# Opening order, score banks and one turn of the first rows in an attention and mixture-of-experts kernel

## The chip, the cores and the metric

The kernel runs as one program on one core of a Trainium2 chip. The metric is device microseconds from launch to end, the median of several executions. TensorE (PE) multiplies and turns tiles, VectorE (DVE) and ScalarE (ACT) work on the results, GpSimd (POOL) helps with elementwise work and starts the indirect transfers, and SyncE (SP) starts nearly all others. Each engine has a list of instructions of its own and takes them in that order.

## The reference

Three stages follow each other, all in float32. Shapes: 4 batches of 576 tokens, 8 heads of 64, so 2304 rows of 512 numbers between the stages.

```python
# windowed attention: a key counts where 0 <= rel < 128
scores = (q @ k.T) / sqrt(64) + slopes[head] * (-abs(rel));  masked: -1e9
attn = exp(scores - max); attn /= sum + 1e-9;  x = attn @ v
# dense layer over 2304 rows, 512 -> 2048 -> 512
h = x @ w_in;  x = (h - tanh(h)) @ w_out
# experts: 8, one for each row, 512 -> 1024 -> 512
xn, en = x / norm(x), expert_emb / norm(expert_emb)
logits = xn @ en.T / tau;  expert = argmax;  gate = softmax[expert]
out = gate * (relu(x @ w1[expert]) @ w2[expert])
```

## The kernel before

The 2304 rows are 18 blocks of 128, two blocks to a group, nine groups. Attention runs by block and, within it, by four quarters of two heads each: scores on PE into two score banks (`sc0`, `sc1`, one for each head), masking, bias and row minimum on DVE (`soft`), the exponential on ACT, then a turn of the probabilities, and the product with the values (`pv`). The first four blocks ("early", 16 quarters) are all float32: their probabilities are turned on PE through the one `misc` bank (`tr_pe`, L526), copied out (`tr_out`) and multiplied by `pv_f` (L540). Block 0 has one key block, so its scores are 128 wide, the others' 256. Later blocks use split operands and a transposing DMA instead (L520, L551).

When a block's four quarters are there, `x_out` turns its 512 numbers per row on PE (L642, four 128x128 turns) and writes a high part (ACT) and a low part (DVE, L655) into one of four `xT` slots. The dense layer runs in steps of two tiles of 128 hidden units: 24 matrix products of 256 columns for the first matrix (`g1`, L695), tanh, subtraction, a split into `gh` and `gl` (two sets of buffers, by the parity of the step), and 12 products of 512 columns for the second (`g2`, L719), which add up in the banks `acc0` and `acc1`. There are 72 steps.

Group 0 is visited twice. In the first visit it does four of its eight steps, since the weights are still arriving; its partial sums go out to memory (`spill`). Then group 1 does all eight, and group 0 comes back for the other four. For that return the kernel before has stored group 0's attention rows in memory (`px`, L651), reads them back (L637) and turns them again (`x_out` with `back=True`).

The order on each engine comes from a planner (`Plan.order`). Every task has an engine or a choice of two, a cost per engine, a due time, and keys that it reads and writes. The planner picks the task that can start first by its own costs; ties go to the earlier due time. It allows only one user of `misc` at a time. What the planner assumes is not what the chip does; only the order that results is in the program.

The opening is set by due times: the bias table's source `tmp` at -20, constants and expert embeddings at -9, then queries, keys and values of block 0. `emb` loads the eight expert embeddings, sums their squares on DVE (`sq`, L269), takes a power on POOL (L285), scales them on DVE (L273 to L275), turns them on PE (L280), copies them out and splits them on POOL. `consts` makes eight bias tables on DVE (L240), one for each head. `qk_early` loads queries and keys of the first four blocks; there the keys of block 1 are loaded for block 1 and again for block 2, and those of block 2 again for block 3, so that two key blocks always lie side by side. `weight` loads a 512 KB weight tile (planned at `WLOAD`) and rebuilds float32 from it on DVE and ACT.

Of the kernel before, what the change touches and what calls it, by code (L numbers as in the profile page):

```python
# [10 lines left out]
F32 = mybir.dt.float32  # L11
# [14 lines left out]
DM = H * D  # L26
FF = 2048
E = 8
# [6 lines left out]
FT = FF // 128  # L35
# [4 lines left out]
NF = 4  # L40
WLOAD = 1.46
LOENG = {"DVE": 0.69}
# [3 lines left out]
N0 = 1  # L46
NPX = 16
ALPHA = 1.0
RATE = 0.5
# [115 lines left out]
class Builder:  # L165
# [64 lines left out]
    def consts(self, P):  # L230
        nc, i = self.nc, self.i
        at = {}

        def tmp(e):
            at[0] = self.at.tile([128, 512], F32, tag="xr", name="tmp", bufs=1)
            nc.sync.dma_start(out=at[0][:, 0:384], in_=i["c_bias"])

        P.add({"SP": 0.55}, tmp, -20, w=[("xr", m) for m in range(4)])
        for h in range(H):
            P.add({"DVE": 0.2}, lambda e, h=h: nc.vector.tensor_scalar(  # L240
                out=self.bias[:, h, :], in0=at[0][:, 0:256], scalar1=2.0 ** -(h + 1), scalar2=None, op0=ALU.mult),
                -20 + h, r=[("xr", 0)], w=[("bias", h)])
        P.add({"POOL": 0.5}, lambda e: nc.gpsimd.tensor_copy(out=self.tri, in_=at[0][:, 256:384]), -11,
              r=[("xr", 0)], w=["tri"])
# [14 lines left out]
    def emb(self, P, due):  # L259
        nc = self.nc  # L260
        ss = self.rt.tile([E, 1], F32, name="ess")

        def load(e):
            self.ec2 = self.at.tile([128, 512], F32, tag="pt0", name="ec", bufs=1)[0:E, :]
            nc.sync.dma_start(out=self.ec2, in_=self.i["emb"])

        def sq(e):
            junk = self.at.tile([128, 512], F32, tag="pt1", name="sq", bufs=1)[0:E, :]
            nc.vector.tensor_tensor_reduce(out=junk, in0=self.ec2, in1=self.ec2, scale=1.0, scalar=0.0,  # L269
                                           op0=ALU.mult, op1=ALU.add, accum_out=ss)  # L270
# [13 lines left out]
        P.add({"DVE": 0.6}, sq, due, r=["ec", ("pt", 0), "at"], w=["ess", ("pt", 1)])  # L284
        P.add({"POOL": 0.6}, lambda e: nc.gpsimd.tensor_tensor(out=ss, in0=ss, in1=self.half[0:E], op=ALU.pow), due,  # L285
              w=["ess"], r=["small"])
        P.add({"DVE": 0.8}, norm, due, w=["ess", "ec"], r=[("pt", 0), "at"])
        P.add({"PE": 0.5}, tr, due, r=["ec", ("pt", 0), "con", "at"], w=["eps"], take="misc")
        P.add({"DVE": 0.1}, lambda e: nc.vector.tensor_copy(
# [17 lines left out]
    def weight(self, P, kind, f, due):  # L307
# [6 lines left out]
        v = {}  # L314
# [18 lines left out]
        def lo(e):  # L333
# [5 lines left out]
                 ("o", FT - 4): [("qf", 2), ("qf", 3)]}.get(key, [])  # L339
        if kind == "o" and 1 <= FT - f < NF:  # L340
            slots = [("kf", FT - f, 0), ("kf", FT - f, 1)]
        P.add({"SP": WLOAD}, load, due - 2, w=[raw] + slots)
# [49 lines left out]
    def qk_early(self, P, b, due):  # L392

        nc, d2 = self.nc, b // 2

        def load_k(e):
            t = max(b, 1)
            if b != 1:
                self.kf[t] = self.wp.tile([128, 2, 4, 128], F32, tag=f"wo{FT - t}", name=f"kf{t}")
# [8 lines left out]
        P.add({"SP": 0.73}, load_q, due, r=["at"], w=[("qf", b)] + ([] if b % 2 else [("qf", b + 1)]))  # L408
        P.add({"SP": 0.73 if b < 2 else 1.46}, load_k, due, r=["at"],
              w=[("kf", 1, 0)] if b == 1 else [("kf", max(b, 1), 0), ("kf", max(b, 1), 1)])  # L410

# [31 lines left out]
    def quarter(self, P, a, due):  # L443
# [11 lines left out]
        sk = (a // 2) % 2  # L455

        def scores(jj):
            sc = v["sc"][jj] = self.scores[jj]
            j = qq + 2 * jj
            hp, p0 = hf * 4 + j, 64 * jj  # L460
            if early:
                x = slice(1, 2) if one else slice(0, 2)
                nc.tensor.matmul(sc[:, 0:W // 128, :], lhsT=self.qf[b // 2][p0:p0 + 64, b % 2, hf * 2 + qq, :],
                                 rhs=self.kf[max(b, 1)][p0:p0 + 64, x, hf * 2 + qq, :], start=True, stop=True)
                return
# [126 lines left out]
        for jj in range(2):  # L592
            if early:
                P.add({"PE": 0.3 if one else 0.42}, lambda e, jj=jj: scores(jj), due,
                      r=["at", ("qf", b)] + [("kf", max(b, 1), x) for x in ([1] if one else [0, 1])], w=[("sc", jj)])
            else:
                P.add({"PE": 0.11 if one else 0.22}, lambda e, jj=jj: scores(jj), due,
                      r=["at"] + ks + [("kl", x, hf) for x in kv] + q, w=[("sc", jj)])
        for jj in range(2):
            P.add({"DVE": ttr}, lambda e, jj=jj: soft(jj), due, r=["at", ("bias", qd * 2 + jj)],  # L600
                  w=[("sc", jj), ("mx", jj, a % 2)])
        for jj in range(2):
            P.add({"ACT": 0.57 if one else 0.67}, lambda e, jj=jj: exp(jj), due,
                  r=["at", ("sc", jj), ("mx", jj, a % 2)], w=[("p32", pb, jj), ("sm", sk, qq, jj)])
        sm = [("sm", sk, x, y) for x in range(2) for y in range(2)]
# [23 lines left out]

    def x_out(self, P, b, s, due, back=False):  # L630

        nc = self.nc
        v = {}

        def reload(e):
            t = self.xr[b] = self.at.tile([128, DM], F32, tag="xr", name="xr", bufs=1)
            nc.sync.dma_start(out=t, in_=self.px[b])  # L637

# [607 lines left out]
    def build(self):  # L1246
# [5 lines left out]
        self.bucket = dp.tile([ROWS, ROW], F32, name="bucket")  # L1252
        self.px = dp.tile([2 * N0, 128, DM], F32, name="px")
        self.pa = dp.tile([2 * N0, 128, DM], F32, name="pa")
# [4 lines left out]
        self.consts(P)  # L1259
        self.small_loads(P, -9)  # L1260
        self.emb(P, -9)
        all_f = list(range(FP))
# [12 lines left out]
        for g, fps in visits:  # L1275
# [226 lines left out]
```

## Time and profile before

| what | value |
|---|---|
| time, median of three runs | 810.32 us (808.01 to 810.85) |
| the profiled execution, its span | 813.71 us, 812.0 us |
| PE, its weight loads | 775.1 us (95%), 684.4 us (84%) |
| DVE, ACT, POOL | 569.6 us (70%), 422.0 us (52%), 227.1 us (28%) |
| data moved | 118.90 MB |

A row of the timeline gives the start in us, the duration in us, the engine, the line in the program, the operation, the result and its operands, their shapes and the number of instructions merged into the row; in brackets stands how long the engine had been idle and whose end let it go on. PE's ends are modelled, and neighbouring products overlap; the price of one is therefore read from its start to the start of the next row. A float32 product is two instructions.

### The profile page before, as it was taken

What the parts mean: (1) busy time and instruction counts of PE and PEld (TensorE: products, weight loads), DVE (VectorE), ACT (ScalarE), POOL (GpSimd) and SP (SyncE); (2) the same over time, 40 slices, a digit from 0 to 9 for tenths busy, and PEclk for the clock granted to TensorE, in tenths of its full rate; (3) what the DMA queues carried; (4) which work ended last, traced back from release to release, by engine and by line L of the source; (5) the groups of instructions that cost most, each with busy time, mean ns of one, the idle gap of its engine ahead of it and who ended that gap; (6) DMA issues with size and microseconds to landing.
All of it is one profiled execution on the core that took longest, in us unless ns stands there. A gap on an engine that the chain in (4) does not pass through costs nothing. (4 is left out here: it accounts for less than half of the span.)

```text
span 812.0 us, 15246 instructions
## 1 busy us (share of the span) xinstructions
PE 775.1 (95%) x5225; PEld 684.4 (84%) x5225; DVE 569.6 (70%) x1544; ACT 422.0 (52%) x953; POOL 227.1 (28%) x242
## 2 busy tenths in 40 slices
PE   6999999988999998999999999989999999999995
PEld 4688998886888987888988989978879899989894
DVE  5788988968587697788787886776456665756420
ACT  4787866555354455555555643555246554545220
POOL 2113034646253145144242422321100211210210
PEclk9999999999999999999999999999999999999998
DMA  8896079666245335445364442474167666655100
GB/s 306 312 365 229 34 211 271 139 129 136 65 93 132 82 86 117 105 98 119 84 130 112 73 79 53 153 211 143 66 217 231 202 208 202 198 184 184 40 29 30
DMA packets 128264, 118.90 MB, mean 146 GB/s; under 512 B 87973, under 2 KB 92069, under 8 KB 128048
## 3 DMA queue, kind: packets, MB, share of 16 engines
q1 hardware_dynamic: 125152, 108.37, 48.7%
q0 software_dynamic: 3024, 9.46, 3.2%
q8 instruction: 43, 0.70, 0.4%
q14 instruction: 45, 0.37, 0.2%
HBM read 86.84 MB, written 17.08 MB: 128 GB/s over the span
## 5 line engine op out<-in xcount | busy, mean ns | idle before, releaser
L695 PE MATMUL h<-xT,wi 128*128 128x256 f32 x1728 | 225.5, 284 | 0.0
L695 PEld LDWEIGHTS h<-xT,wi 128*128 128x128 f32 x1728 | 217.0, 191 | 5.9 <-issue 1.3
L719 PE MATMUL acc<-wo,gh 128*128 128x512 f32 x576 | 184.8, 402 | 0.3 <-DVE x2row L759 0.3
L719 PE MATMUL acc<-wo,gl 128*128 128x512 f32 x288 | 113.8, 395 | 0.0
L719 PEld LDWEIGHTS acc<-wo,gh 128*128 128x128 f32 x576 | 100.0, 189 | 15.1 <-DVE x2row L759 0.5
L700 ACT ACTIVATE t<-h 128x512 f32<-128x512 f32 x72 | 43.1, 599 | 103.2 <-PE h L695 98.2
L1129 PE MATMUL y<-eo,ge 128*128 128x512 f32 x336 | 88.8, 399 | 0.5 <-ACT ge L1110 0.5
L505 ACT ACTIVATE p<-sc,mx 128x256 f32<-128x256 f32 (+1 forms) x128 | 59.3, 465 | 41.5 <-DVE mx L491 37.7
L1154 POOL DMA_INDIRECT out<-yo,ix x23 | 24.4, 1059 | 188.1 <-ACT yo L1150 39.8
L491 DVE CUSTOM_DVE_ANT_0 sc<-sc,bias 128x256 f32<-128x256 f32 (+1 forms) x144 | 52.6, 371 | 28.5 <-PE sc L469 19.6
L1129 PEld LDWEIGHTS y<-eo,ge 128*128 128x128 f32 x336 | 59.5, 188 | 10.8 <-ACT ge L1110 0.8
L712 DVE TENSOR_TENSOR gl<-t,gh 128x512 fp32r<-128x512 f32 x72 | 64.9, 902 | 4.9 <-ACT gh L708 4.3
L1027 DVE TENSOR_TENSOR eo<-est,eo 128x512 fp32r<-128x512 f32 x61 | 44.9, 738 | 28.8 <-ACT eo L1023 28.1
L719 PEld LDWEIGHTS acc<-wo,gl 128*128 128x128 f32 x288 | 54.4, 189 | 12.6 <-DVE gl L712 0.5
L1023 ACT CAST eo<-est 128x512 fp32r<-128x512 f32 x64 | 39.6, 620 | 37.1 <-PE y L1125 21.3
L1116 DVE SCALAR_TENSOR_TENSOR ge<-he,ge 128x256 fp32r<-128x256 f32 x104 | 28.7, 316 | 41.2 <-ACT ge L1110 41.2
L1094 PEld LDWEIGHTS he<-xA,ei 128*128 128x128 f32 x384 | 54.2, 188 | 2.5
L1094 PE MATMUL he<-xA,ei 128*128 128x288 f32 (+2 forms) x384 | 56.1, 295 | 0.0
L703 DVE TENSOR_TENSOR t<-h,t 128x512 f32<-128x512 f32 x72 | 49.4, 686 | 9.3 <-ACT t L700 9.1
L1110 ACT ACTIVATE ge<-he 128x288 fp32r<-128x288 f32 (+2 forms) x56 | 23.1, 415 | 62.9 <-PE he L1094 58.7
L1094 PEld LDWEIGHTS he<-xT,ei 128*128 128x128 f32 x384 | 53.4, 189 | 2.1
L1094 PE MATMUL he<-xT,ei 128*128 128x288 f32 (+2 forms) x384 | 54.8, 295 | 0.0
(202 smaller groups left out, 1312.1 us busy)
## 6 DMA issues: line engine op xcount, KB each, us to landing
est<-in_w SPq DMA_DIRECT2D x128, 256.0 KB, 3.2
rawi<-in_w_in SPq DMA_DIRECT2D x16, 511.8 KB, 6.9
rawo<-in_w_out SPq DMA_DIRECT2D x16, 511.8 KB, 5.0
stk<-in_k SPq DMA_DIRECT2D x30, 256.0 KB, 2.9
stq<-in_q SPq DMA_DIRECT2D x28, 256.0 KB, 3.1
bucket<-in_c_pad SPq DMA_DIRECT2D x8, 771.0 KB, 6.3
xe<-bucket SPq DMA_DIRECT2D x17, 257.0 KB, 3.5
vst<-in_v SPq DMA_DIRECT2D x30, 128.0 KB, 2.4
```

The costliest lines, as they stand in the source:

```text
L491: nc.vector.tensor_tensor_reduce(out=x, in0=x, in1=self.bias[:, h, c0:c1], scale=-0.125, scalar=mx[:, 1:2] if m else 3.0e38, op0=ALU.add, ...
L505: nc.scalar.activation(out=v["p32"][:, jj * W:(jj + 1) * W], in_=x, func=AF.Exp, scale=-1.0, bias=v["mx"][jj][:, 0:1], accum_out=self.sums ...
L695: nc.tensor.matmul(h3(v["h"], f2), lhsT=w[:, a, k, :], rhs=xT[c][:, :, k, :], start=(k == 0 and n == 0), stop=(k == KD - 1 and n == 2))
L700: nc.scalar.activation(out=v["t"], in_=v["h"].rearrange("p a b -> p (a b)"), func=AF.Tanh)
L703: nc.vector.tensor_tensor(out=v["t"], in0=v["h"].rearrange("p a b -> p (a b)"), in1=v["t"], op=ALU.subtract)
L712: self.eng(e).tensor_tensor(out=v["gl"], in0=v["t"], in1=v["gh"].bitcast(F32), op=ALU.subtract)
L719: nc.tensor.matmul(self.acc[g, t], lhsT=v[a][:, c0:c0 + 128], rhs=self.w["o", fs[f2]][:, c, :], start=(first and f2 == 0 and n == 0), stop ...
L1023: nc.scalar.copy(out=t[:, 0, :], in_=v["x"])
L1027: self.eng(eng).tensor_tensor(out=t[:, 1, :], in0=v["x"], in1=t[:, 0, :].bitcast(F32), op=ALU.subtract)
L1094: nc.tensor.matmul(h[:, 0:N], lhsT=w[:, a, c0:c0 + 128], rhs=xT()[b][:, k, 0:N], start=(k == 0 and n == 0), stop=(k == KD - 1 and n == 2))
L1116: nc.vector.scalar_tensor_tensor(out=g[:, o:o + c1 - c0], in0=hk[f][:, c0:c1], scalar=0.0, in1=g[:, c0:c1].bitcast(F32), op0=ALU.max, op1= ...
L1129: nc.tensor.matmul(y[t], lhsT=gt(f, a)[:, (t - ts[0]) * 128:(t - ts[0] + 1) * 128], rhs=self.w["o", f0 + f][:, b, :], start=(f == 0 and n ...
```

## The change

Seven edits stand together.

1. Group 0's rows are turned once. The `xT` slots of its first visit are still intact at its return, so the store, the reload and the second turn go.
2. The first queries and keys are loaded first (due -25), ahead of `tmp`; the constants come with due -19.
3. `emb` is no longer called at the start but in the loop over blocks, behind `x_out` of block 0, with due 0. Its scratch is now the `gh` and `gl` buffers of odd steps. The call stands under `if b == 0`, not under `if g not in seen`.
4. Two bias tables stay on DVE; the other six go to POOL.
5. In the first eight quarters every second one has its scores in the banks `acc0` and `acc1`.
6. The early keys are loaded once each. Block 1 and 3 still find their two key blocks side by side; block 2 does not, so each of its eight score products becomes two of 128 columns.
7. `WLOAD` goes from 1.46 to 1.28, and some buffer keys follow the new key layout.

```diff
-WLOAD = 1.46
+WLOAD = 1.28
+NALT = 8
...
-            P.add({"DVE": 0.2}, lambda e, h=h: nc.vector.tensor_scalar(
+            P.add({"DVE": 0.2} if h < 2 else {"POOL": 0.5}, lambda e, h=h: self.eng(e).tensor_scalar(
...
-            self.ec2 = self.at.tile([128, 512], F32, tag="pt0", name="ec", bufs=1)[0:E, :]
+            self.ec2 = self.m1.tile([128, 512], F32, tag="gh1", name="ec", bufs=1)[0:E, :]
...
-        P.add({"SP": 0.2}, load, due, w=["ec", ("pt", 0)], r=["at"])
+        ec = [("gh", 1), ("gl", 1)]
+        P.add({"SP": 0.2}, load, due, r=[("xT", 0)], w=ec)
...
-            for x in ([b] if b < 2 else [b, b - 1]):
-                nc.sync.dma_start(out=self.kf[t][:, t - x], in_=self.i["k0"][x])
+            nc.sync.dma_start(out=self.kf[d2][:, 1 - b % 2], in_=self.i["k0"][b])
...
+        P.add({"SP": 0.73}, load_q, -25 if b == 0 else due, r=["at"], w=both("qf"))
+        P.add({"SP": 0.73}, load_k, -25 if b == 0 else due, r=["at"], w=both("kf"))
...
+        bank = "acc" if a < NALT and a % 2 else "sc"
+
         def scores(jj):
-            sc = v["sc"][jj] = self.scores[jj]
+            sc = v["sc"][jj] = self.scores[jj] if bank == "sc" else self.psA.tile(
+                [128, 2, 128], F32, tag=f"acc{jj}", name="scx", bufs=1)
...
+                kt = [self.kf[x // 2][p0:p0 + 64, 1 - x % 2, hf * 2 + qq, :] for x in ([b] if one else [b, b - 1])]
+                if b % 2 and not one:
+                    kt = [self.kf[b // 2][p0:p0 + 64, :, hf * 2 + qq, :]]
+                for m, k in enumerate(kt):
+                    out = sc[:, 0:2, :] if b % 2 and not one else sc[:, m, :]
+                    nc.tensor.matmul(out, lhsT=self.qf[b // 2][p0:p0 + 64, b % 2, hf * 2 + qq, :], rhs=k, start=True,
+                                     stop=True)
...
-        if back:
-            P.add({"SP": 0.73}, reload, due - 2, r=["at", ("px", b)], w=xr)
-        elif b < 2 * N0:
-            P.add({"SP": 0.73}, lambda e: nc.sync.dma_start(out=self.px[b], in_=self.xr[b]), due, r=["at"] + xr,
-                  w=[("px", b)])
...
-        self.emb(P, -9)
+        self.small_loads(P, -19)
...
-                self.x_out(P, b, sl[n], -5 if g in seen else d0 + 4 * rate, g in seen)
+                if g not in seen:
+                    self.x_out(P, b, sl[n], d0 + 4 * rate)
+                if b == 0:
+                    self.emb(P, 0)
```

On PE the program opens so before (`sc` are the score banks, `p` and `p32x` the probabilities of even and odd quarters, `of` the product with the values):

```order
L463 MATMUL sc_97<-kf_135,qf_132 128x128
L463 MATMUL sc_98<-kf_135,qf_132 128x128
L463 MATMUL sc_97<-kf_135,qf_132 128x128
L280 MATMUL misc<-con,ec 128x8 x4
L463 MATMUL sc_98<-kf_135,qf_132 128x128
L526 MATMUL misc<-con,p_167 128x128 x2
L463 MATMUL sc_97<-kf_135,qf_132 128x128
L540 MATMUL of<-vf_140,ptf 128x128 x2
L526 MATMUL misc<-con,p32x 128x128 x2
L463 MATMUL sc_98<-kf_135,qf_132 128x128
```

And so now, with `scx` for the banks that it borrows:

```order
L470 MATMUL sc_97<-kf_132,qf_130 128x128
L470 MATMUL sc_98<-kf_132,qf_130 128x128
L470 MATMUL scx<-kf_132,qf_130 128x128 x2
L470 MATMUL sc_97<-kf_132,qf_130 128x128
L533 MATMUL misc<-con,p_160 128x128 x2
L470 MATMUL sc_98<-kf_132,qf_130 128x128
L470 MATMUL scx<-kf_132,qf_130 128x128 x2
L547 MATMUL of<-vf_138,ptf 128x128 x2
L533 MATMUL misc<-con,p32x 128x128 x2
L470 MATMUL sc_97<-kf_132,qf_130 128x256
```

The turn of the embeddings has gone from here. The second quarter's scores follow the first's at once, and the first turn of probabilities has one head's scores of the third quarter ahead of it.

On POOL the opening reads so before (the row named ISA stands where the trace shows MODIFY_POOL_CONFIG, a setting-up of POOL; `tri` is a constant, `ess` the embeddings' norms):

```order
L253 MEMSET thr 1x8 x16
L243 CAST tri<-tmp 128x128
L285 ISA
L285 TENSOR_TENSOR ess<-ess,half 8x1
L297 CAST en_89<-enT 128x4x8
```

And so now:

```order
L254 MEMSET thr 1x8 x16
L241 ISA
L241 TENSOR_SCALAR bias<-tmp 128x256 x6
L244 CAST tri<-tmp 128x128
L371 TENSOR_TENSOR khl<-stk,khl 64x512 x2
```

The setup row stands ahead of the six bias tables, and the power has moved behind other work.

In group 0's second visit PE has this behind the first GEMM of its third step now; the rows before hold no L280 there:

```order
L693 MATMUL h<-xT_65,wi_1192 128x256
L693 MATMUL h<-xT_64,wi_1192 128x256
L281 MATMUL misc<-con,ec 128x8 x4
L476 MATMUL sc_97<-khl,qst_1634 128x256 x2
L476 MATMUL sc_98<-khl,qst_1634 128x256 x2
L693 MATMUL h<-xT_64,wi_1246 128x256
```

So the embeddings are loaded, normalised and turned a second time. From the second half of step 30 (of 0 to 71) to the end of the program PE's order is the same in both kernels.

## Rows read from the trace of the kernel before

**Rows 1.** Windows: stretch, then busy us of PE, PEld, DVE, ACT, POOL; PEclk; DMA.

```profile
10.16:31.81 21.65, 20.71 (x76) 14.27 (x76) 12.76 (x47) 12.71 (x39) 4.73 (x8) 1.00 0.96 360
41.28:100.00 58.72, 58.72 (x397) 51.57 (x396) 51.79 (x107) 47.68 (x100) 10.10 (x9) 1.00 0.57 213
199.90:205.90 6.00, 4.29 (x24) 3.36 (x24) 2.54 (x6) 0.62 (x1) 1.47 (x1) 0.72 0.02 5
```

**Rows 2.** Timeline of all engines, the opening until the first exponentials.

```profile
0.86 0.40 SPq L236 DMA_DIRECT2D tmp<-in_c_bias  x1
1.78 0.43 SPq L401 DMA_DIRECT2D kf<-in_k  x1
...
3.35 1.80 DVE L240 TENSOR_SCALAR bias<-tmp 128x256 bf16<-128x256 f32 x8 [1.28 <-DMA tmp<-in_c_bias]
...
6.57 0.68 DVE L269 CUSTOM_DVE_ANT_0 sq<-ec 8x512 f32<-8x512 f32 x1 [1.42 <-DMA ec<-in_emb]
...
7.18 0.28 DVE L491 CUSTOM_DVE_ANT_0 sc<-sc,bias 128x128 f32<-128x128 f32 x1
...
7.92 0.36 ACT L505 ACTIVATE p<-sc,mx 128x128 f32<-128x128 f32 x1
```

**Rows 3.** Timeline of PE alone, from the first scores to the 34th microsecond.

```profile
5.76 0.80 PE L463 MATMUL sc<-kf,qf 64*128 64x128 f32 x4 [5.76 <-DMA kf<-in_k]
...
8.92 0.59 PE L280 MATMUL misc<-con,ec 8*128 8x8 f32 x4
...
10.16 0.69 PE L526 MATMUL misc<-con,p 128*128 128x128 f32 x2
...
12.51 0.64 PE L526 MATMUL misc<-con,p32x 128*128 128x128 f32 x2
13.08 0.80 PE L463 MATMUL sc<-kf,qf 64*128 64x128 f32 x4
13.81 1.22 PE L540 MATMUL of<-vf,ptf 128*128 128x128 f32 x4
14.82 0.63 PE L526 MATMUL misc<-con,p 128*128 128x128 f32 x2
...
24.13 1.09 PE L526 MATMUL misc<-con,p 128*128 128x128 f32 x4 [0.78 <-DVE xT L655]
...
26.30 2.07 PE L540 MATMUL of<-vf,ptf 128*128 128x128 f32 x8
28.16 1.06 PE L526 MATMUL misc<-con,p32x 128*128 128x128 f32 x4
29.15 1.23 PE L463 MATMUL sc<-kf,qf 64*128 64x256 f32 x4
30.31 1.86 PE L540 MATMUL of<-vf,ptf 128*128 128x128 f32 x8
32.01 0.60 PE L526 MATMUL misc<-con,p 128*128 128x128 f32 x4
```

**Rows 4.** POOL: its setup and power by line, then groups: count, busy, mean ns.

```profile
L285 POOLq MODIFY_POOL_CONFIG  x2: 1/1/1, 3.7 to 3.8; - x2
...
L285 POOL TENSOR_TENSOR ess<-ess,half 8x1 f32<-8x1 f32 x1 | 0.6, 582 | 3.6 <-DVE ess L269 3.6
L369 POOL TENSOR_TENSOR khl<-stk,khl 64x512 fp32r<-64x512 f32 x2 | 2.5, 1270 | 10.7 <-ACT khl L365 10.7
L436 POOL TENSOR_TENSOR vst<-vst,vt 128x256 f32<-128x256 f32 x2 | 1.3, 673 | 7.8 <-ACT vt L434 7.8
```

**Rows 5.** Timeline of PE at group 0's second turn of rows.

```profile
76.53 0.60 PE L642 MATMUL misc<-con,xr 128*128 128x128 f32 x4
76.89 3.11 PE L695 MATMUL h<-xT,wi 128*128 128x256 f32 x24
```

**Rows 6.** Waits of SP's queue: who waited for whom, us in total, times, longest.

```profile
SPq L520 <- DVE ph L515: 74.4, 23, 7.3
...
SPq L651 <- DVE xr L581: 12.4, 2, 7.8
```

More of the change, by code (lines that the diff above doesn't have):

```diff
@@ L263, in load @@
         def load(e):
[L264 removed]
+            self.ec2 = self.m1.tile([128, 512], F32, tag="gh1", name="ec", bufs=1)[0:E, :]
             nc.sync.dma_start(out=self.ec2, in_=self.i["emb"])
         def sq(e):
[L268 removed]
+            junk = self.m1.tile([128, 512], F32, tag="gl1", name="sq", bufs=1)[0:E, :]
             nc.vector.tensor_tensor_reduce(out=junk, in0=self.ec2, in1=self.ec2, scale=1.0, scalar=0.0,
@@ L281, in tr @@
                                     self.ident[0:E, 0:E])
-        P.add({"SP": 0.2}, load, due, w=["ec", ("pt", 0)], r=["at"])
-        P.add({"DVE": 0.6}, sq, due, r=["ec", ("pt", 0), "at"], w=["ess", ("pt", 1)])
+        ec = [("gh", 1), ("gl", 1)]
+        P.add({"SP": 0.2}, load, due, r=[("xT", 0)], w=ec)
+        P.add({"DVE": 0.6}, sq, due, w=["ess"] + ec)
         P.add({"POOL": 0.6}, lambda e: nc.gpsimd.tensor_tensor(out=ss, in0=ss, in1=self.half[0:E], op=ALU.pow), due,
               w=["ess"], r=["small"])
-        P.add({"DVE": 0.8}, norm, due, w=["ess", "ec"], r=[("pt", 0), "at"])
-        P.add({"PE": 0.5}, tr, due, r=["ec", ("pt", 0), "con", "at"], w=["eps"], take="misc")
+        P.add({"DVE": 0.8}, norm, due, w=["ess"] + ec)
+        P.add({"PE": 0.5}, tr, due, r=["con"] + ec, w=["eps"], take="misc")
         P.add({"DVE": 0.1}, lambda e: nc.vector.tensor_copy(
@@ L339, in weight @@
                  ("o", FT - 4): [("qf", 2), ("qf", 3)]}.get(key, [])
-        if kind == "o" and 1 <= FT - f < NF:
-            slots = [("kf", FT - f, 0), ("kf", FT - f, 1)]
+        if kind == "o" and FT - f <= 2:
+            slots = [("kf", 2 * (FT - f) - 2), ("kf", 2 * (FT - f) - 1)]
         P.add({"SP": WLOAD}, load, due - 2, w=[raw] + slots)
@@ L396, in load_k @@
         def load_k(e):
-            t = max(b, 1)
-            if b != 1:
-                self.kf[t] = self.wp.tile([128, 2, 4, 128], F32, tag=f"wo{FT - t}", name=f"kf{t}")
-            for x in ([b] if b < 2 else [b, b - 1]):
-                nc.sync.dma_start(out=self.kf[t][:, t - x], in_=self.i["k0"][x])
+            if b % 2 == 0:
+                self.kf[d2] = self.wp.tile([128, 2, 4, 128], F32, tag=f"wo{FT - 1 - d2}", name=f"kf{d2}")
+            nc.sync.dma_start(out=self.kf[d2][:, 1 - b % 2], in_=self.i["k0"][b])
         def load_q(e):
@@ L406, in load_q @@
             nc.sync.dma_start(out=self.qf[d2][:, b % 2], in_=self.i["q0"][b])
-        P.add({"SP": 0.73}, load_q, due, r=["at"], w=[("qf", b)] + ([] if b % 2 else [("qf", b + 1)]))
-        P.add({"SP": 0.73 if b < 2 else 1.46}, load_k, due, r=["at"],
-              w=[("kf", 1, 0)] if b == 1 else [("kf", max(b, 1), 0), ("kf", max(b, 1), 1)])
+        both = lambda kind: [(kind, b)] + ([] if b % 2 else [(kind, b + 1)])
+        P.add({"SP": 0.73}, load_q, -25 if b == 0 else due, r=["at"], w=both("qf"))
+        P.add({"SP": 0.73}, load_k, -25 if b == 0 else due, r=["at"], w=both("kf"))
     def v_full(self, P, b, due):
@@ L594, in quarter @@
                 P.add({"PE": 0.3 if one else 0.42}, lambda e, jj=jj: scores(jj), due,
-                      r=["at", ("qf", b)] + [("kf", max(b, 1), x) for x in ([1] if one else [0, 1])], w=[("sc", jj)])
+                      r=["at", ("qf", b)] + [("kf", x) for x in ([b] if one else [b, b - 1])], w=[(bank, jj)])
             else:
                 P.add({"PE": 0.11 if one else 0.22}, lambda e, jj=jj: scores(jj), due,
-                      r=["at"] + ks + [("kl", x, hf) for x in kv] + q, w=[("sc", jj)])
+                      r=["at"] + ks + [("kl", x, hf) for x in kv] + q, w=[(bank, jj)])
         for jj in range(2):
             P.add({"DVE": ttr}, lambda e, jj=jj: soft(jj), due, r=["at", ("bias", qd * 2 + jj)],
-                  w=[("sc", jj), ("mx", jj, a % 2)])
+                  w=[(bank, jj), ("mx", jj, a % 2)])
         for jj in range(2):
             P.add({"ACT": 0.57 if one else 0.67}, lambda e, jj=jj: exp(jj), due,
-                  r=["at", ("sc", jj), ("mx", jj, a % 2)], w=[("p32", pb, jj), ("sm", sk, qq, jj)])
+                  r=["at", (bank, jj), ("mx", jj, a % 2)], w=[("p32", pb, jj), ("sm", sk, qq, jj)])
         sm = [("sm", sk, x, y) for x in range(2) for y in range(2)]
@@ L628, in quarter, with x_out @@
             P.add({"DVE": 0.5, "POOL": 0.7}, mul, due, r=["at"] + sm, w=half)
-    def x_out(self, P, b, s, due, back=False):
+    def x_out(self, P, b, s, due):
         nc = self.nc
         v = {}
-        def reload(e):
-            t = self.xr[b] = self.at.tile([128, DM], F32, tag="xr", name="xr", bufs=1)
-            nc.sync.dma_start(out=t, in_=self.px[b])
         def tr(e):
```

5 lines of the change are left out of this document (removed).

## Prediction

> **What bounds the kernel now.** I read the windows by stage first. Between 41 and 100 us TensorE is busy for 58.72 of 58.72 us and VectorE for 51.79, so there the end is pushed by TensorE's work alone [rows 1]. The opening is different. From 10.16 to 31.81 us TensorE is busy for 20.71 of 21.65 us, yet it works at half pace: four turns take 1.06 us at 28.16 and 0.60 us at 32.01 [rows 1, 3]. That is the lower of its two levels (1.2 and 2.4 GHz) until about 31.8; the window's clock column reads 1.00 there nevertheless, so here the durations have to tell it. Third, the start: TensorE waits 5.76 us for the first keys, and the first turn of probabilities, from which it has no large gap any more, comes at 10.16 [rows 3]. So three things can move the end: when the gap-free work begins, when the clock rises, and how much work TensorE has. From the middle of step 30 on its order is unchanged. What the new kernel is ahead by then it should keep.
>
> **The start.** Loads go out one after the other: `tmp` first at 0.86, landing by 3.35 (2.5 us), the keys third at 1.78, landing by 5.76 (4.0 us) [rows 2, 3]. Now queries and keys have the first two places and `tmp` the third. For the second place I take 2.9 us, nearer to the first; issued at about 1.3 the keys land at 4.2 (bounds 3.8 and 5.3). `tmp` in third place lands at 1.78 + 2.5 at the earliest and 1.78 + 4.0 = 5.8 at the latest; it is smaller than the keys, I take 5.5. Then softmax waits for `tmp`, not for TensorE. In front of it VectorE made eight tables in 1.80 us, 0.225 each, and squared the embeddings from 6.57 to 7.18, where the first softmax began [rows 2]. Now two tables stand there: 5.5 + 0.45 = 5.95, 1.2 us sooner. The second exponential ends 1.1 us behind the first softmax (7.92 + 0.36 against 7.18) [rows 2], so at 7.05. The first turn followed 3 us behind the first softmax, as both heads of the second quarter and the embeddings stood ahead of it and waited in turn for the one pair of banks. Now one score product stands ahead, which needs the first exponential only. I put the first turn at 7.6 (bounds 7.05 and, if every landing is late, 8.6) instead of 10.16.
>
> **POOL's tables.** No row shows POOL multiplying a 128x256 tile by a number. Its nearest are 0.67 us for a 128x256 subtraction and 1.27 us for one of 64x512 [rows 4]. I take 0.67: the six tables are ready from 6.2 to 9.5, always before the quarter that needs them. At 1.27 the last is there at 5.5 + 7.6 = 13.1, and its turn of probabilities in the list below stands at 16. So both ends cost at most some tenths in a wait for banks. The setup in front of them was reached at 3.7 before, and the power behind it ran as soon as VectorE let it, 3.6 us later [rows 4]: the setup took at most 3.6 us. Now POOL comes to it at about 1.7, so it is over by 5.3, before `tmp`. The Trainium skill (GPSIMD Engine Reference, section 2.1) says that the first call behind such a setup pays about 6 us for loading code. By that the power could not have run before 9.7, so the trace disagrees; if it held, the first table would begin at 7.7 and the sum below would shrink by about 1.2 us.
>
> **TensorE's list to the same point.** I take as the point the end of the fifth quarter after the first (the product with the values that ends at 32.0 [rows 3]). Prices at the low level, start to start: two turns 0.57, 128-wide scores 0.73 for a pair and taken the same for one head, a product with values 1.01 (two key halves: 1.86), four turns 0.99, 256-wide scores 1.16 [rows 3]. From the first turn on the new order holds 4 x 0.57, scores 2 x 0.73 + 5 x 1.16, products 4 x 1.01 + 2 x 1.86, four turns 2 x 0.99 and block 0's turn of rows 0.99: 20.3 us. 7.6 + 20.3 = 27.9, against 32.0: 4.1 us ahead at the same clock. The wait for `misc` of 0.78 us at 24.13 [rows 3] goes, because between block 0's turn of rows and the next user of the bank stand now a product and a quarter's scores. The masks, copies and weights on VectorE and ScalarE hide beside this: they are busy for 12.8 and 12.7 of 21.65 us [rows 1].
>
> **Transfers.** Two key blocks, two stores and two reloads go, 256 KB each. TensorE waited for none of these. The stores held SP's list, though: 7.8 us for the second [rows 6], with weights queued behind it. Weights therefore come earlier. I cost this at nothing in time, since TensorE has no wait for a weight in any row I read; it only gives VectorE work earlier. `WLOAD` changes the order and nothing else.
>
> **What is added.** Block 2's scores are cut in two: two pairs of 128 at 0.73 instead of a pair of 256 at 1.16, +0.3 us at the low level, half of that at the high one. Four quarters, the first of them slow: +0.9 (bounds 0 and, if each half cost a whole 256-wide one, 4 x 1.16 = 4.6; the nearest row is the 128-wide pair). The embeddings' turn took 0.59 us in idle time [rows 3]; now it stands twice in dense time at the high level: 2 x 0.3 = +0.6. Group 0's second turn of rows goes: 0.36 us for each of two blocks [rows 5], -0.7.
>
> **The sum.** -4.1 + 0.9 + 0.6 - 0.7 = -3.3 us. The profiled execution took 813.7, so 810.4 under the profiler; its like, the median of the runs shown, lies 3.4 lower at 810.3, and from that I forecast 807.0. Between steps 4 and 30 attention and dense layer are interleaved otherwise than before, around waits such as the one in the stretch from 199.9 to 205.9, where the clock averages 0.72 [rows 1]. I expect as much waiting as before there, and give it 2 us either way.
>
> **Rivals.**
> - *The clock rises early.* Before the rise TensorE had worked with no gap above 0.2 us since 24.13, on 256-wide scores, turns of four and products [rows 3]. In the new list a like mix begins at about 11 and has no gap. If the clock rose at 20, the 7.9 us from there to 27.9 would take half: 4 us more, 803.0. Against it: single-head scores, turns and cut scores lie between, and the old kernel stayed low through a like mix.
> - *The clock rises at the same time as before, not at the same work.* Then the 4.1 us gained are worth 2.05: 809.1. For it: from 10.16 to 24.13, nearly without gaps, the clock stayed low [rows 3].
> - *Slower: the embeddings' second round.* The call stands in the loop without the test for a first visit, so the change does not only move the embeddings, it does them twice. The second round takes the buffers `gh` and `gl` of odd steps in the middle of dense work; its load starts when step 11 has left them, and PE, VectorE and POOL each have a piece of it in order. The chain is a landing (2.5 us) and 2.9 us from squares to turned (6.57 to 8.92 + 0.59) [rows 2, 3], 5.4 together. TensorE has two whole first GEMMs of 3.1 us [rows 5] and more between, so nothing waits if SP issues the load at once. But SP works in order and its longest wait for VectorE is 7.3 us [rows 6], with the transposing transfers of attention around. Behind the squares on VectorE queue the reductions of attention, the next `gl` and the second-half copies, on which TensorE waits in turn. From 0.8 us of delay on TensorE can begin to wait. At the full 7.3 it loses 6.5 and, as in the stretch at 199.9, a fall of the clock worth 0.28 x 6.0 = 1.7: 807.0 + 8.2 = 815.2. The time is above the old one from 3.3 us of loss on.
>
> **How the numbers follow.** The forecast with its own range of 805 to 809 has a chance of 0.42, the early clock 0.22 (801 to 805), the late clock 0.22 (808 to 811), the second round 0.14 (809 to 816). The range that leaves 2 in 10 out is 801.5 to 813.0; the bounds of the landing (1 us), of the middle steps (2 us) and of the cut scores (3.7 more: 810.7) lie inside. A measurement of this kernel can tell 0.5%, 4.05 us, from no change, so faster means below 806.3 and slower above 814.4. Below 806.3 lie nearly all of the early clock and almost half of the forecast, 0.40; above 814.4 part of the second round and what I have not seen, 0.07; the rest, 0.53, is between.
>
> **What would show it.** In the new profile: the first scores at 4 to 5 us and the first softmax near 6, with VectorE let go by `tmp`; the first turn of probabilities near 7.6; turns of four falling from about 1.06 to 0.60 us at a time that says which clock case holds (20, 28 or 32); the first GEMM of step 0 a few us before 41.3; no L642-like turn at 76 and 80; four small turns of embeddings twice; and from step 31 on the same gaps as before, shifted. I am wrong if TensorE waits between the opening's products for tables, exponentials or values, if it waits at the second round of embeddings, or if the lead at step 4 is gone by step 31.

## The result, and the profile after

The changed kernel takes 798.48 us (median of four, 795.44 to 801.22) against 809.2 us (the median of four now): a ratio of 0.9861, 95% interval 0.9824 to 0.9898. Run once more beside the kernel before it stood at 798.93 us and 0.9865 (0.9841 to 0.989). It is about 11 us faster (10.7 and 11.0). The forecast was 807.0, and the range ended at 801.5.

The windows of the new profile, cut where TensorE starts the first GEMM of step 0, 12, 30 and 71 (columns as in [rows 1]):

```profile
0.00:35.03 35.03, 25.03 (x160) 19.19 (x161) 25.66 (x90) 24.11 (x70) 13.13 (x38) 1.00 0.95 354
35.03:119.52 84.49, 84.26 (x579) 74.99 (x578) 75.24 (x174) 65.96 (x141) 22.17 (x23) 1.00 0.62 202
119.52:251.46 131.94, 128.55 (x980) 113.83 (x979) 111.88 (x313) 72.91 (x186) 68.69 (x71) 1.00 0.60 141
251.46:534.14 282.68, 277.89 (x2050) 249.21 (x2048) 220.05 (x612) 146.89 (x344) 99.74 (x94) 0.99 0.47 110
534.14:793.80 259.66, 247.21 (x1476) 220.93 (x1474) 136.55 (x351) 109.98 (x214) 35.33 (x33) 0.99 0.46 147
```

The third stretch of the kernel before, of a second profile of it, and of a second profile of the changed kernel:

```profile
126.68:266.00 139.32, 131.97 (x977) 116.87 (x976) 109.07 (x316) 73.78 (x187) 64.95 (x65) 0.98 0.58 135
```

```profile
124.12:261.62 137.50, 131.86 (x976) 117.56 (x975) 108.96 (x316) 73.43 (x187) 65.11 (x65) 0.96 0.58 137
```

```profile
122.17:254.82 132.65, 128.57 (x981) 113.83 (x979) 111.83 (x313) 72.94 (x186) 68.64 (x71) 1.00 0.58 135
```

From step 12 to step 30 TensorE waited 7.3 and 5.6 us before (length less busy time) and 3.4 and 4.1 us after. The clock column stood at 0.98 and 0.96 and stands at 1.00. As the mean of two profiles each, the stretch went from 138.4 to 132.3 us: 6.1 us less. Who held TensorE up there, before (second profile) and after (first profile; us in total, times, longest):

```profile
PE o L551 <- DMA pt<-ph: 4.0, 3, 3.2
PE misc L642 <- DVE xr L584: 0.6, 1, 0.6
PE sc L469 <- ACT p L505: 0.6, 1, 0.6
PE misc L807 <- DMA x3T<-x: 0.4, 1, 0.4
```

```profile
PE o L558 <- DVE gl L710: 1.1, 1, 1.1
PE misc L805 <- DMA x3T<-x: 0.7, 1, 0.7
PE acc L717 <- DVE x2row L757: 0.5, 1, 0.5
PE misc L805 <- DVE xT L653: 0.5, 1, 0.5
PE o L558 <- DMA pt<-ph: 0.3, 1, 0.3
```

The wait of 3.2 us is the one to look at. TensorE's timeline before (second profile), and the same place in a second profile of the changed kernel:

```profile
174.74 0.63 PE L469 MATMUL sc<-khl,qst 128*128 128x256 f32 x4
175.20 1.59 PE L695 MATMUL h<-xT,wi 128*128 128x256 f32 x12
180.02 1.25 PE L551 MATMUL o<-vt,pt 128*128 128x192 bf16 x8 [3.23 <-DMA pt<-ph]
181.03 1.20 PE L469 MATMUL sc<-khl,qst 128*128 128x256 f32 x4
182.03 1.34 PE L642 MATMUL misc<-con,xr 128*128 128x128 f32 x4
183.16 1.27 PE L551 MATMUL o<-vt,pt 128*128 128x192 bf16 x8
185.01 1.25 PE L469 MATMUL sc<-khl,qst 128*128 128x256 f32 x4 [0.58 <-ACT p L505]
186.34 1.22 PE L719 MATMUL acc<-wo,gh 128*128 128x512 f32 x2
```

```profile
175.19 0.96 PE L476 MATMUL sc<-khl,qst 128*128 128x256 f32 x4
176.66 0.73 PE L717 MATMUL acc<-wo,gh 128*128 128x512 f32 x2 [0.51 <-DVE x2row L757]
...
178.86 0.60 PE L645 MATMUL misc<-con,xr 128*128 128x128 f32 x4
179.29 0.72 PE L558 MATMUL o<-vt,pt 128*128 128x192 bf16 x8
179.82 0.72 PE L717 MATMUL acc<-wo,gh 128*128 128x512 f32 x2
```

The window of the low clock in that second profile of the kernel before:

```profile
179.23:189.47 10.24, 8.77 (x35) 7.03 (x36) 7.39 (x26) 6.39 (x17) 7.21 (x8) 0.50 0.75 173
```

Before, a product with the values, scores, a turn of rows, another such product and scores stand in a row, with the second GEMM behind them. The first finds its turned probabilities on the way, TensorE idles 3.23 us, and the granted clock lies at its lower level from 179.2 to 189.5: scores take 1.20 us, not 0.63 as at 174.74. Now pieces of the second GEMM stand between them, no wait is longer than 0.51 us, and the clock stays up. The mean granted clock of each execution shows that this is no accident of one profile. The column counts the opening as 1.00, so one less the clock, times the span, is what falls cost at most: 9.1 us on average over 98 executions of the kernel before, 4.0 over nine of the changed one. About 3 us of each are the last 5 to 8 us of the program, which stand at the lower level with TensorE idle.

The rest of the gain is smaller, or not shown to be one. Steps 0 to 12 take 85.4 and 85.6 us before, 84.5 and 84.2 after. Steps 30 to 71 take 285.4 and 285.8 us before, 282.7 and 282.4 after. But the same two orders with some products put ahead of them (`b_warm` and `a_warm` below) gave 282.1 and 285.1 there, so no gain of the order is shown behind step 30.

The opening moved as forecast, but it is not where the time is. The first scores run at 4.34 us (forecast 4.2), the first softmax at 6.36 (5.95), the first turn at 7.97 (7.6). The rows are TensorE's, with one of POOL and one of VectorE:

```profile
4.34 0.80 PE L470 MATMUL sc<-kf,qf 64*128 64x128 f32 x4 [4.34 <-DMA kf<-in_k]
...
5.80 5.47 POOL L241 TENSOR_SCALAR bias<-tmp 128x256 bf16<-128x256 f32 x6 [4.06 <-DMA tmp<-in_c_bias]
...
6.36 0.28 DVE L498 CUSTOM_DVE_ANT_0 sc<-sc,bias 128x128 f32<-128x128 f32 x1
...
7.25 0.79 PE L470 MATMUL sc<-kf,qf 64*128 64x128 f32 x2 [1.68 <-ACT p L512]
7.97 0.69 PE L533 MATMUL misc<-con,p 128*128 128x128 f32 x2
...
12.33 0.68 PE L470 MATMUL scx<-kf,qf 64*128 64x256 f32 x2
12.94 0.71 PE L547 MATMUL of<-vf,ptf 128*128 128x128 f32 x4
...
23.08 1.16 PE L547 MATMUL of<-vf,ptf 128*128 128x128 f32 x8 [1.32 <-ACT ptf L537]
24.08 0.60 PE L533 MATMUL misc<-con,p 128*128 128x128 f32 x4
25.50 0.71 PE L470 MATMUL sc<-kf,qf 64*128 64x128 f32 x4 [0.82 <-ACT p L512]
```

In this profile the clock rose at 12.5 us, and the products behind it take about half as long. The second profile of the very same program has the same rows up to 12.3, starting within 0.03 us, and then:

```profile
12.30 1.06 PE L470 MATMUL scx<-kf,qf 64*128 64x256 f32 x2
13.29 1.22 PE L547 MATMUL of<-vf,ptf 128*128 128x128 f32 x4
...
19.65 1.06 PE L533 MATMUL misc<-con,p 128*128 128x128 f32 x4
...
26.89 0.60 PE L533 MATMUL misc<-con,p 128*128 128x128 f32 x4
```

There it rose at 21.3. The kernel before rose at 31.8 in the profile of the prediction, and at 18.8 in its second. With the rises at 18.8 and 21.3, step 0 begins at 38.56 and 37.99: a lead of 0.6 us, with the rise 2.5 us later in the changed kernel.

### The profile page after: what moved, and what is told of

It reads as the page before. It is cut to its first block, busy times and chain, and to the rows that moved or that the text cites. A ratio compares the mean times of both kernels' runs of the same rounds, so it can differ in the third digit from the quotient of the medians.

```text
span 793.8 us, 15243 instructions
## 1 busy us (share of the span) xinstructions
PE 762.9 (96%) x5237; PEld 678.1 (85%) x5237; DVE 569.4 (72%) x1538; ACT 419.8 (53%) x953; POOL 239.1 (30%) x256
## 4 chain that ended last, share of the span: by engine, by line
PE 61%; DMA 13%; DVE 11%; issue 9%; ACT 2%; POOL 1%; SPq 1%; POOLq 0%; DVEq 0%; ACTq 0%
PE h L693 18%; PE acc L717 16%; PE he L1092 9%; PE y L1127 7%; DMA out<-yo,ix 4%; PE o L558 3%; PE y L1123 2%; DMA rawo<-in_w_out 2%; PE sc L476 2%; DMA x3T<-x 2%; DVE gl L710 2%; DMA est<-in_w 2%; DMA pt<-ph 1%; DMA stk<-in_k 1%; DVE sc L498 1%
## 5 line engine op out<-in xcount | busy, mean ns | idle before, releaser
L710 DVE TENSOR_TENSOR gl<-t,gh 128x512 fp32r<-128x512 f32 x72 | 67.5, 937 | 5.7 <-ACT gh L706 4.8
L1127 PEld LDWEIGHTS y<-eo,ge 128*128 128x128 f32 x336 | 59.5, 188 | 10.6 <-ACT ge L1108 0.6
L498 DVE CUSTOM_DVE_ANT_0 sc<-sc,bias 128x256 f32<-128x256 f32 (+1 forms) x136 | 49.5, 373 | 23.7 <-PE sc L476 20.0
L717 PEld LDWEIGHTS acc<-wo,gl 128*128 128x128 f32 x288 | 54.1, 188 | 12.7 <-DVE gl L710 0.7
L522 POOL TENSOR_TENSOR ph<-p,ph 128x512 f16<-128x512 f32 (+1 forms) x33 | 38.3, 1160 | 56.9 <-ACT ph L517 41.6
```

The lines of the kernel that those rows point to most:

```text
L498: nc.vector.tensor_tensor_reduce(out=x, in0=x, in1=self.bias[:, h, c0:c1], scale=-0.125, scalar=mx[:, 1:2] if m else 3.0e38, op0=ALU.add, ...
L522: self.eng(e).tensor_tensor(out=ph[:, 2 * W:4 * W], in0=v["p32"][:, 0:2 * W], in1=ph[:, 0:2 * W], op=ALU.subtract)
L710: self.eng(e).tensor_tensor(out=v["gl"], in0=v["t"], in1=v["gh"].bitcast(F32), op=ALU.subtract)
L717: nc.tensor.matmul(self.acc[g, t], lhsT=v[a][:, c0:c0 + 128], rhs=self.w["o", fs[f2]][:, c, :], start=(first and f2 == 0 and n == 0), stop ...
L1127: nc.tensor.matmul(y[t], lhsT=gt(f, a)[:, (t - ts[0]) * 128:(t - ts[0] + 1) * 128], rhs=self.w["o", f0 + f][:, b, :], start=(f == 0 and n ...
```

## The experiments

Eighteen runs were made, each timed against the kernel before on the same chip (an edit is against the kernel that the name begins with: `b` before, `a` changed). "12 to 30" is the time from step 12's first GEMM to step 30's, "30 to 71" the next stretch, each in one profile.

| kernel | us | ratio (95%) | 12 to 30 | 30 to 71 |
|---|---|---|---|---|
| before, three profiles (one of them b_warm) | 808.1 to 809.9 | 1 | 136.3 to 139.3 | 282.1 to 285.8 |
| changed, two profiles | 798.5, 798.9 | 0.9861, 0.9865 | 131.9, 132.7 | 282.7, 282.4 |
| b_nopx | 801.5 | 0.9895 (0.986 to 0.993) | 132.0 | 282.5 |
| b_lat | 799.6 | 0.988 (0.985 to 0.991) | 134.3 | 276.6 |
| a_px | 806.4 | 0.9974 (0.995 to 0.9999) | 138.6 | 283.9 |
| a_pxghost | 803.2 | 0.9934 (0.9908 to 0.996) | 138.6 | 280.3 |
| a_wl120 | 796.0 | 0.9843 (0.9803 to 0.9884) | 130.1 | 280.5 |
| a_wl136 | 806.5 | 0.9958 (0.9933 to 0.9982) | 137.3 | 285.8 |
| a_wl146 | 801.1 | 0.9918 (0.9884 to 0.9952) | 137.1 | 284.9 |
| a_tmp1st | 802.4 | 0.993 (0.9902 to 0.9957) | 136.9 | 281.8 |
| a_noalt | 804.8 | 0.9951 (0.9932 to 0.9971) | 134.3 | 283.7 |
| a_emb1 | 796.5 | 0.9849 (0.981 to 0.9888) | 129.4 | 287.2 |
| a_embghost | 800.3 | 0.9889 (0.9859 to 0.9919) | 131.8 | 285.0 |
| a_emb1_wl120 | 801.0 | 0.9894 (0.9859 to 0.9929) | 129.1 | 289.0 |
| a_warm | 800.4 | 0.9874 (0.9848 to 0.9901) | 131.6 | 285.1 |
| a_lat | 799.6 | 0.9879 (0.9853 to 0.9906) | 138.1 | 276.6 |
| a_emb1_lat1 | 800.2 | 0.9881 (0.9856 to 0.9906) | 141.8 | 276.4 |

**Is the clock's rise part of the change?** Both kernels again, without an edit:

> The kernel before, unchanged, profiled a second time. Theory A (the rise of the clock is set by the order of the opening): the clock rises near 32 us again, within 2 us, and the first GEMM of step 0 starts near 41. Theory B (the moment of the rise is chance): it lies elsewhere, anywhere between 10 and 35 us, and the first GEMM moves with it by half of that. The same look tells whether the waits between 179 and 206 us and the two falls of the clock there belong to this order (they come again) or to that one execution. Time by both: 808 to 811 us as median, ratio 1.00.

> The changed kernel, unchanged, profiled a second time. Theory A: the clock rises at 12 to 14 us again and the first GEMM of step 0 starts near 35. Theory B: the rise lies elsewhere between 10 and 30 us. Lead over the kernel before at the start of step 21 again 12 to 15 us if the order of the steps 15 to 21 is what took the waits away, 6 to 9 if it was that execution. Time by both 796 to 801 us, ratio 0.985 to 0.990.

The rises lay at 18.8 and 21.3: theory B. The wait and the fall at 180 us came again in `b_again`; the fall at 202.5 did not. Neither came in `a_again`, whose lead at step 21 was 10.6 us, in neither of the two ranges expected. Then products of ones were put ahead of all work (`b_warm` ten, `a_warm` seven):

```diff
+            t = self.vt[:, 0, 0:4, :].rearrange("p h d -> p (h d)")
+            nc.vector.memset(t, 1.0)
+            for n in range(10):
+                nc.tensor.matmul(self.misc(), lhsT=t[:, 0:128], rhs=t[:, 128:640], start=True, stop=True)
             for fn, e in P.order({"misc": 1}):
```

> The kernel before with ten products of ones (128x512, bf16) put ahead of everything on TensorE, between about 1.4 and 5.7 us, where it only waits for keys; their result is never read. Theory A (the clock is most of the gain): the clock rises before 12 us, the stretch to 31.8 takes half the time where TensorE is the bound, the first GEMM of step 0 comes 5 to 9 us sooner and the time falls by 4 to 9 us: 801 to 806, ratio 0.989 to 0.995. Rival C (the gain lies in the order of the steps behind the opening, the waits of 179 to 206 us): the rise may come sooner, but the end moves by less than 2 us, ratio 0.998 to 1.002.

> The changed kernel with seven such products ahead of its first scores. Theory A: the clock was up by 12.5 us already and the opening then waits for exponentials and copies, not for TensorE, so at most the 8 us from 4.3 to 12.5 gain half of their busy time, 2 us, and likely under 1: 797 to 799, ratio 0.984 to 0.988. Theory B (chance): the products fix an early rise in every execution, the mean falls by 2 to 4 us and the runs spread less: 794 to 797.

The ten took 6.37 us from 1.85, so that the first scores came 2.4 us late, at 8.15. The rise came at 19.1 and 21.5 and the times moved by nothing (0.9984, 0.9962 to 1.0006) and +1.4. For `a_warm` that is outside both ranges of time, though its ratio (0.9874) is in theory A's. Work ahead did not bring the rise, so this could not price an early one. In all profiles the rise lay between 12.5 and 31.8, whatever the edit.

**Which edit carries it?** Four were undone or mended one at a time:

```diff
-WLOAD = 1.28
+WLOAD = 1.46
```

> The changed kernel with WLOAD back at 1.46. Three looks at the kernel before and its copies showed 49 to 51 us between the starts of steps 15 and 21 (4 us of waits and 2 to 4 us lost at the low clock), the changed kernel 45 to 46 us (1.3 to 1.8 us of waits, no fall). Theory W (the planned price of a weight's load sets the order of SP's list there, and with it the late transposing transfer): the stretch is at 48 to 51 us again and the time 4 to 6 us above the changed kernel, 803 to 805, ratio 0.992 to 0.996. Rival P (it is the store, reload and second turn of group 0's rows): the stretch stays at 45 to 46 us, 798 to 800, ratio 0.985 to 0.988.

For `a_px` the store, the reload and the second turn of edit 1 came back, as in the diff's removed lines:

> The changed kernel with group 0's store, reload and second turn of rows put back (two stores, two reloads, eight 128x128 turns). Theory P: steps 15 to 21 take 48 to 51 us again, and the time rises by 4 to 7 us to 803 to 806, ratio 0.992 to 0.996. Rival W: 45 to 46 us there; only the turns' 0.7 us come back, 799 to 800.5, ratio 0.986 to 0.989.

```diff
-                if b == 0:
+                if b == 0 and g not in seen:
                     self.emb(P, 0)
```

> The changed kernel with the embeddings done once: the call stands under a test for group 0's first visit. By the prediction's sum the second round costs 0.3 us of TensorE, and no wait for it shows in the trace: 798 to 799, ratio 0.984 to 0.988. Rival (the second round holds back the lists of SP and VectorE in group 0's return, from step 12 on): 2 us or more less, below 797. Third way (steps 15 to 21 are a matter of the whole order, and any edit shuffles them): 47 us or more there, and a time 2 to 6 us higher.

```diff
-        P.add({"SP": 0.73}, load_q, -25 if b == 0 else due, r=["at"], w=both("qf"))
-        P.add({"SP": 0.73}, load_k, -25 if b == 0 else due, r=["at"], w=both("kf"))
+        P.add({"SP": 0.73}, load_q, due, r=["at"], w=both("qf"))
+        P.add({"SP": 0.73}, load_k, due, r=["at"], w=both("kf"))
```

> The changed kernel with queries and keys of block 0 behind the bias table's source again (their due is no longer -25). The prediction gave the opening's new loads 1.2 us of a softmax that begins sooner. If that holds, the first softmax comes at 7 us or later, and the first GEMM 1 to 2 us later at a like rise of the clock: 799 to 801, ratio 0.986 to 0.990. Rival (the opening's lead is used up by step 0, where TensorE waits for exponentials and copies): less than 0.5 us either way, 798 to 799.5. Steps 15 to 21 at 45 to 46 us by both.

Three different edits, undone (`a_wl146`, `a_px`, `a_tmp1st`), cost 2.2, 7.5 and 3.5 us, or 4.3, 8.8 and 5.3 by the ratios on their own chips; the interval of the first still overlaps that of the changed kernel. All three brought back the same thing: 137 to 139 us from step 12 to 30. `a_emb1` came out below 797, as its rival said, and not at 798 to 799. For `a_tmp1st` both theories had expected a short stretch there; both missed. That edit moves two loads in the opening, and the stretch lies 120 us behind them. So the suspicion fell on the order. Edits 4 and 6 were not undone alone.

**Order or work?** The order of `a_px` with its additional tasks empty (the edit is shown against `a_px`, cut; the copies behind the second turn are left out too), edit 1 alone in the kernel before, and two values of a number that adds no instruction:

```diff
-            t = self.xr[b] = self.at.tile([128, DM], F32, tag="xr", name="xr", bufs=1)
-            nc.sync.dma_start(out=t, in_=self.px[b])
+            pass
...
         def tr(e):
+            if back:
+                return
...
-            P.add({"SP": 0.73}, lambda e: nc.sync.dma_start(out=self.px[b], in_=self.xr[b]), due, r=["at"] + xr,
+            P.add({"SP": 0.73}, lambda e: None, due, r=["at"] + xr,
```

> The order of the kernel with group 0's store, reload and second turn put back (806 us, 27.1 and 27.6 us for steps 15 to 17 and 18 to 20), but with these tasks empty: the planner places them, and nothing is issued for them; every other instruction stands as in that kernel. Theory O (what cost the 7 us was the order that the planner then finds for the steps up to 30): the time stays at 804.5 to 806.5, less only the turns' 0.7 us, ratio 0.994 to 0.998, and steps 18 to 20 wait for 3 us or more again. Rival P (it was the work itself, the stores and reloads on SP's list and the shared buffers): 798 to 800, ratio 0.986 to 0.989, 25 us or less for steps 18 to 20.

> The kernel before with edit 1 alone: group 0's rows are turned once, no store, no reload. Theory P: the gain of the changed kernel lies in this edit, 5 to 8 us: 801 to 804, ratio 0.990 to 0.994. Theory O: 0.7 us for the turns and whatever the new order happens to give, up to 5 us either way; steps 18 to 20 need not take less than 28 us.

> The changed kernel with WLOAD at 1.20 in place of 1.28. No instruction is added or taken away, only the order differs. Theory O: orders that differ by such a number scatter by several us with no trend; steps 15 to 23 wait anywhere from 1 to 7 us, and the time lies between 796 and 806, following that wait and any fall of the clock behind it. Theory W (1.28 is better for a reason, a nearer price of a load): the time moves smoothly from 801.1 at 1.46 by 798.9 at 1.28, so 797.5 to 799 here.

> The changed kernel with WLOAD at 1.36. Theory O: as for 1.20, anywhere from 796 to 806. Theory W: between the times at 1.28 and 1.46, 799 to 800.5.

Of the 7.5 us that `a_px` lost, 4.3 stay lost when nothing is issued for it (5.6 of 8.8 by the ratios). TensorE's list is the same in both but for the eight turns, and steps 12 to 30 take 138.6 us with the work and without it, 18 to 20 take 27.6. `a_pxghost` issues what the changed kernel issues (two instructions went from POOL to VectorE), which takes 132.3 there; so in this stretch the order alone makes 6 us. Theory O holds for the larger part, though 803.2 lies between the ranges of both theories. What makes up the other 3.2 was not settled (the two intervals overlap): the turns are 0.7 of it, and in the two profiles the difference lies behind step 30 (283.9 and 280.3), where none of these tasks stands. `b_nopx` came out as theory P said, 7 us faster, though by a shorter stretch from 12 to 30 with steps 18 to 20 as long as before (27.7 against 28.0). Steps 0 to 12, where the second turn of rows stood, take 84.2 us in it against 85.4, but other orders without that turn range from 83.2 to 86.3. `WLOAD` at 1.20, 1.28, 1.36 and 1.46 gives 796.0, 798.9, 806.5 and 801.1: no trend, 10 us of spread, and the same work. The stretch from 12 to 30 does not order all times by itself: `a_emb1_wl120` has the shortest (129.1) and takes 801.0 us, `a_emb1_lat1` the longest (141.8) and takes 800.2.

**The order alone.** The planner is told that every transfer lands 1.5 us later than it believed; all the work of the kernel before remains:

```diff
-    LAT = {"PE": 0.3, "SP": 0.0, "SW": 0.0}
+    LAT = {"PE": 0.3, "SP": 1.5, "SW": 0.0}
```

> The kernel before with all its work, only the planner's belief changed: every transfer lands 1.5 us later than it assumed. Theory O (the loss of the kernel before lies in an order that lets TensorE's list reach products with the values, turns of rows and second GEMMs too early): TensorE then has more dense work ahead of them, steps 12 to 30 take 134 us or less in place of 136 to 139, and the time falls by 3 to 8 us to 801 to 806. Rival (those waits go back to work that edit 1 takes away): 137 us or more there, 807 or more. An order that turns out worse elsewhere, in the opening or behind step 30, would show as a shorter stretch without a shorter time.

799.6 us, below the 801 to 806 expected: one number in the planner gives the kernel before what the seven edits gave, with no work taken away. But it is another gain in the main. The stretch from 12 to 30 stands between the two kernels at 134.3 us, with 3.2 us of waits and one fall left. Most lies beyond it, where TensorE hardly waits any more (length less busy time 1.1 us, from 8.3 and 7.4):

```profile
125.60:259.85 134.25, 131.09 (x989) 117.27 (x987) 105.57 (x308) 74.05 (x187) 66.17 (x62) 0.97 0.61 136
259.85:536.47 276.62, 275.52 (x2048) 248.18 (x2047) 216.29 (x616) 149.39 (x351) 103.14 (x94) 1.00 0.48 111
```

The last stage, from step 71 on, gave back some 4 us (264.2 against 259.4 to 260.7). The remaining questions on single edits (in `a_embghost` the second round is planned and not issued):

> The changed kernel's order with the tasks of the second embedding round left empty: placed by the planner, nothing issued. By the prediction the round costs TensorE 0.3 us and nothing else: 798 to 799.5, ratio 0.985 to 0.988. If it holds back VectorE, POOL or SP in the return of group 0, 796 to 797.5. The kernel with a single round in an order of its own took 796.5, so what is left between the two is the order's.

> The changed kernel without borrowed score banks (NALT 0). The prediction put the first turn of probabilities 2.6 us sooner, in part by these banks, and it came 2.2 us sooner. If that lead counts at the end: 1 to 2.5 us slower, 800 to 801.5. If the lead of the opening is used up by the start of step 0 anyway, the time follows the stretch from step 12 to 30 alone: 132 us or less there goes with 796 to 801, 136 or more with 801 to 806.

> The changed kernel with the embeddings done once and WLOAD at 1.20, the two edits that came out best alone (796.5 and 796.0). If each has a worth of its own, they add up: 793 to 794.5, ratio 0.980 to 0.983. Theory O: they are two orders out of many, and their union is a third: anywhere from 794 to 804, to be read from the stretch of steps 12 to 30 (129 to 139 us).

The second round costs nothing that can be measured in this order: left empty it gives 800.3 against 798.9, above both ranges expected. So the 796.5 of `a_emb1` are not shown to be the round's price. In `a_noalt` the round does cost: TensorE stands 3.11 us before it, and at the low clock behind it.

```profile
140.55 0.72 PE L476 MATMUL sc<-khl,qst 128*128 128x256 f32 x4
144.38 0.59 PE L281 MATMUL misc<-con,ec 8*128 8x8 f32 x4 [3.11 <-DVE ec L276]
144.90 5.49 PE L693 MATMUL h<-xT,wi 128*128 128x256 f32 x24
```

24 products take 5.49 us where 3.1 is usual [rows 5]. Step 0 of `a_noalt` starts at 36.66 with the rise at 20.8, so the borrowed banks bring no lead there. The two best edits did not add up (801.0, not 793 to 794.5). That kernel has 9.4 us of waits and two falls behind step 30, the changed one 4.8 and 5.9 us with one fall and none. Last, the belief in the changed kernel, and with one round:

> The changed kernel with the planner's belief that every transfer lands 1.5 us later. If both gains are the same one (fewer waits between steps 12 and 30): 798 to 801, ratio 0.986 to 0.990. If the belief takes away the waits behind step 30 as well, as it did in the kernel before (276.6 us from step 30 to 71 in place of 282 to 286, less 2 to 4 us that the last stage lost): 793 to 797, ratio 0.980 to 0.985. Scatter of orders by itself: 796 to 806.

> The changed kernel with one embedding round and a belief of 1.0 us. If the waits on both sides of step 30 go (130 us or less from step 12 to 30, 279 or less from 30 to 71): 790 to 795, ratio 0.976 to 0.983, faster than both kernels. Scatter of orders by itself: 796 to 806.

The waits behind step 30 went (276.6 and 276.4), but those from 12 to 30 came back (138.1 and 141.8), and both ended at 800, with a last stage 2 to 3 us longer. No version is clearly faster than the changed kernel; 796.0 (`a_wl120`) and 796.5 (`a_emb1`) have intervals that overlap its own. Eight of the eighteen times lie outside every range that was expected for them (`a_warm`, `a_wl146`, `a_px`, `a_tmp1st`, `a_pxghost`, `a_wl136`, `b_lat`, `a_embghost`), by 0.4 to 1.4 us.

## Why the prediction was wrong

- **The step that failed** is the sentence that between steps 4 and 30 as much waiting was to be expected as before, "and give it 2 us either way". The stretch from 12 to 30 alone brought 6.1 us: 2.8 of waits and 3.9 at the low clock as the mean of two profiles each, with 0.5 us more work. Rows to see it stood in the prediction: the clock of 0.72 at 199.9 [rows 1], and the waits ahead of the transposing transfers on SP (L520, 74.4 us) [rows 6]. They were taken as a property of the kernel, and they are one of its order: `a_pxghost` takes 138.6 us there for the work that the changed kernel does in 132.3, and the four values of `WLOAD` give 130.1 to 137.3. A bound of 2 us had no row behind it.
- **The opening**, -4.1 us: the times of its first steps were right within 0.4 us, and in a list at the low clock the lead is there: the first turn of four starts at 19.65, against 24.13 [rows 3], with one quarter's scores more ahead of it and block 0's turn of rows behind it. It did not reach step 0. When the clock is up, TensorE waits for exponentials and copies (1.32, 0.82 us), which the prediction itself named as a sign of being wrong, and the wait for `misc` that was to go stands at 0.41 and 0.58 us. The lead at step 0 is 0.6, and by an estimate up to 1.3 more (half of the 2.5 us between the rises) at a like rise. With the first loads of edit 2 undone step 0 starts at 37.59 (rise at 22.3), with edit 5 undone at 36.66 (20.8): no later than in the changed kernel. With VectorE and ScalarE at 12.8 and 12.7 of 21.65 us the prediction called them hidden; at the high clock TensorE waits for them.
- **The clock rivals** (early, 803; late, 809) treated the rise as a consequence of the list. It differed by 9 and 13 us between two executions of one program, so neither could be tested. The rise is not the cause of the gain: with it at 18.8 the kernel before took 808.5 us, and with it at 21.3 the changed one 798.9.
- **POOL's tables** took 0.85 to 0.95 us each, between the bounds of 0.67 and 1.27. VectorE waited 1.8 us for them in all; no run takes this edit back alone. The setup row now stands at 1.7 us and the first table starts at 5.80, just behind `tmp`. The Trainium skill (GPSIMD Engine Reference, section 2.1) says that the first call to freshly loaded code behind such a setup pays about 6 us. Here it was under 4.1, and at most 3.6 in the kernel before, so the trace disagrees.
- **The second round** does no harm in this order, as the sum had it. The rival's mechanism is real, with a shorter wait and a dearer fall than it had: in `a_noalt` 3.1 us of wait, not 6.5, and 2.4 us more for the 24 products behind it, not 1.7.
- **Edit 1** had been costed at -0.7 us and its transfers at nothing. Alone it is worth 7 us (`b_nopx`). In the changed kernel at least 4.3 of the 7.5 us that its return costs come with the order alone, since the tasks need not even do anything; the same split for the kernel before was not run.

## What to carry to other kernels

Where a planner makes the order, the price of an edit is first of all the order that comes out: compare it with one or two neutral changes of the planner's numbers before a gain is put down to the edit. Look for places where TensorE's list has several instructions with long chains behind each other; waits of 2.1 to 3.2 us there were followed by falls of the clock that cost 1.7 to 4.4 us more (half of what TensorE worked in them). And a term for "about as before" needs a row for its bounds like any other.

## What was unexpected of the hardware

The moment of the clock's first rise is not set by the program alone: 31.8 and 18.8 us in two executions of the kernel before, 12.5 and 21.3 in two of the changed one, with the same order and starts within 0.4 us up to the earlier rise. Ten products of 512 columns ahead of all other work did not bring it (19.1). The Trainium skill (TensorE: Matmul & The Clock Gate, section "What you observe") gives half a microsecond either way from run to run for products issued back to back. Here it was 9 to 13 us in an opening of mixed work. What decides it stays open. Against that, the falls at 182.0, 179.2 and 179.6 us came in the same place of the list in all three profiles of the order before (one of them `b_warm`), each in or just behind a wait of 2.1 to 3.2 us.
